# Reordering work around the second chunk of a fused local-attention and gated feed-forward kernel

## The chip, the cores and the metric

The kernel runs on one core of a Trainium2 chip. Its engines are named here as in the profile: PE is TensorE's matmul side and PEld its weight loads, DVE is VectorE, ACT is ScalarE, POOL is GpSimd, SP is SyncE, which here does nothing but issue DMAs. The metric is the device time of one execution in microseconds (us); less is better.

## The reference

Attention over 8 batches, 8 heads, 576 positions and a head width of 64, with a local window and 8 global positions, is followed by a gated feed-forward layer over the 4608 tokens:

```python
scores = scale * np.matmul(q, k.transpose(0, 1, 3, 2))
mask = np.abs(pos[:, None] - pos[None, :]) <= window        # window = 32
mask = mask | is_global[:, None] | is_global[None, :]
attn = softmax(np.where(mask, scores, -1e9))
x = (attn @ v) as 4608 x 512
gelu = 0.5 * g * (1.0 + erf(g * inv_sqrt2))                 # g = x @ w_gate
ffn_out = gelu * (x @ w_val) @ w_out
res_gate = 1.0 / (1.0 + np.exp(-(x @ w_res)))
out = x + res_gate * ffn_out
```

## The kernel before, in words

**Chunks.** The 4608 tokens are cut into 9 chunks of 512 (c = 0 to 8). A chunk is 8 windows of 64 positions, or 4 tiles of 128 tokens (t = 0 to 3). A batch has 9 windows, so chunk c begins in batch c or c-1 and the work for batch b = c + 1 is prepared while chunk c's feed-forward runs. All orders are written out by hand: each engine executes its instructions in the order in which the Python code emits them, so "ahead of" and "behind" below mean places in an engine's own queue. Semaphores are set where one engine's instruction needs another's result or buffer.

**Feed-forward of a chunk.** For each of 12 column blocks j, `ffn_in(c, j)` forms two products of 4 matmuls each (`g_ps`, `v_ps`, L628), takes the Gelu on ACT (L634) and multiplies on DVE (`ht`, L635). Then `ffn_out(c, t)` has, for each of the 4 tiles, a `gate` (4 matmuls into `r_ps`, L646, and a Tanh on ACT into `rsb`, L649) and three `third`s (4 matmuls each into `f_ps`, L671); the last third ends with a DVE step `prb` (L675), a POOL step `ob` (L677) and the DMA of the result from SP (L679).

**Attention of the next chunk, in between.** `scores(c, quad, pps)` forms the scores of four windows and half of the heads (`heads`, L532), takes their exponentials on ACT (`weigh`, L539) and returns a function `mask` that multiplies by the window mask on DVE into `pt` (L555). For chunk 1 alone the exponentials stay in the PSUM bank of the scores (`stay`), and the mask step is what empties that bank. `global_scores(b)`, `global_exp(b)` and `global_rows(b)` treat the 8 global positions of a batch: the last one forms `sn` on PE (L507, L510) from `ptg` and spreads it on DVE into `vgs` (L512). `values(c, t)` forms `nd` for one tile (`local_values`, L573, then the global part from `gt` and `vgs`, L585) and divides on DVE into `xtok` (L591 and L592 for halves, L597 and L598 for whole tiles). `turn_x` transposes `xtok` into `xt`, on PE (L608) or by a DMA from SP (L604).

**PSUM.** Pool `psm` (tag "mm") has four banks that are handed out in turn; `g_ps`, `v_ps`, `r_ps`, `f_ps` and the scores of the second half of the heads share them. Pool `pss` has two banks (scores of the first half of the heads, transposes). Pool `psn` has one buffer of two banks for `sg`, `sn` and `nd`, so a new `nd` waits until the DVE has read the one before.

**Order at the end of chunk 0.** In the last block of the code chunk 1's attention is woven into chunk 0's `ffn_out` by hand: two score groups of quad 0 around `global_scores(1)`, `global_exp(1)`, the gates of tiles 0 and 1 each with its Tanh, the scores of quad 1 and the two other gates alternating, `global_rows(1)`, and the last masks. Then come `values(1, t)` and the thirds. The q and k of batch 2 come in as fp32 into spare space (`load_second`) and are cast to `k_st` on ACT and to `q_st` on POOL (`cast_second`, L205): one piece, then two, then two more of `q_st` at three places among the thirds. `turn_qk(2, "k")` transposes `k_st` into `kt` by DMAs from SP (L466).

**Order at the start of chunk c.** `turn_qk(b)` issues on SP the DMA transposes of `q_st` into `qt` and `k_st` into `kt`; `load_v(b)` (L99) issues five DMAs from POOL's queue; and for c = 1, 2 and 4 `gather` (L328) issues three indirect DMAs from POOL's queue, which fetch the global rows of a pair of batches into `kgf`, `qgf` and `vgf`. At block j = 8 `load_qk(b + 1)` (L91) issues ten DMAs from POOL's queue into `q_st` and `k_st`, each of which waits until the transposes have read its place. In odd chunks, at blocks 8 and 9, `double_qk` (L397), `turn_globals` (L407) and `spread_v` (L435) use what was gathered: pair 1 in chunk 1, pair 2 in chunk 3, pair 3 in chunk 5. At j = 11 `global_scores(b)` uses `qt` and `kt` (`sg` L472, `ss` L481).

**Batch 0.** `local_values(0, 0)` and `local_values(0, 1)` are emitted ahead of `global_rows(0)`; `values(0, 0)` and `values(0, 1)` behind it add the global part.

Of the kernel before, what the change touches and what calls it, by code (L numbers as in the profile page):

```python
# [12 lines left out]
ACTF = mybir.ActivationFunctionType  # L13
# [3 lines left out]
def view(t, p0, pn, off, dims):  # L17

    step = t.ap[0][0]
    return bass.AP(tensor=t.tensor, offset=t.offset + p0 * step + off, ap=[[step, pn]] + dims)  # L20
# [3 lines left out]
def kernel(  # L24
# [12 lines left out]
    nc = tc.nc  # L37
# [459 lines left out]
    def global_rows(b):  # L497

        e = b % 2
        if b:  # L500
            sn = psn.tile([128, 2, 512], F32, name="sn", tag="nd")[:, 0, 0:2 * VG]
        else:
            sn = pss.tile([128, 2 * VG], F32, name="sn", tag="sc")
        for c in range(-1, 5):
            for p in range(NP):
                if c < 0:
                    nc.tensor.matmul(sn[32 * p:32 * p + 32, :], own[e][:, 32 * p:32 * p + 32],  # L507
                                     view(vgb, 0, 128, (b // 2) * VG, [[0, 2], [1, VG]]), start=True, stop=False)
                else:
                    nc.tensor.matmul(sn[32 * p:32 * p + 16, :], ptg[e][:, c, 16 * p:16 * p + 16],  # L510
                                     ve[e][:, c, 2 * p:2 * p + 2, :], start=False, stop=(c == 4))
        nc.vector.tensor_tensor(view(vgs, 0, 128, e * H * VG, [[2 * VG, NP], [VG, 2], [1, VG]]),  # L512
                                view(sn, 0, 128, 0, [[0, NP], [VG, 2], [1, VG]]),
                                view(head8, 0, 128, 0, [[2, NP], [1, 2], [0, VG]]), ALU.mult)


    def first_scores(quad, pp):
# [102 lines left out]
    def ffn_steps(c, j):  # L620
# [15 lines left out]

        return {"g": product("g", wg_t), "v": product("v", wv_t), "end": end}

    def ffn_out(c, t):

        held = {}

        def gate():
            r_ps = psm.tile([128, 512], F32, name="r_ps", tag="mm")
            for kk in range(NKT):
                nc.tensor.matmul(r_ps, xt[c % 2][:, kk, 128 * t:128 * t + 128], wr_t[:, kk, :],  # L646
                                 start=(kk == 0), stop=(kk == NKT - 1))
            held["r"] = work.tile([128, 512], BF16, name="rsb", tag="rsb", bufs=4)
            nc.scalar.activation(held["r"], r_ps, ACTF.Tanh, bias=0.0, scale=0.5)  # L649

        def ending():

            r0 = 512 * c + 128 * t
            for c0, c1 in ((0, 256), (256, 384), (384, 512)):
                f = psm.tile([128, 512], F32, name="f_ps", tag="mm")
                for j in range(NFF):
                    nc.tensor.matmul(f[:, 0:c1 - c0], ht[:, j, 128 * t:128 * t + 128], wo_t[:, j, c0:c1],
                                     start=(j == 0), stop=(j == NFF - 1))
                prb = work.tile([128, 512], F32, name="prb", tag="prb")
                nc.vector.scalar_tensor_tensor(prb[:, c0:c1], held["r"][:, c0:c1], 1.0, f[:, 0:c1 - c0],  # L660
                                               ALU.add, ALU.mult)
                ob = work.tile([128, 512], F32, name="ob", tag="ob", bufs=4)
                nc.vector.tensor_tensor(ob[:, c0:c1], prb[:, c0:c1], xtok[c % 2][:, t, c0:c1], ALU.add)
                nc.sync.dma_start(out[r0:r0 + 128, c0:c1], ob[:, c0:c1])

        def third(n):
            def emit():
                if n == 0:
                    held["f"] = psm.tile([128, 512], F32, name="f_ps", tag="mm")
                for j in range(4 * n, 4 * n + 4):  # L670
                    nc.tensor.matmul(held["f"], ht[:, j, 128 * t:128 * t + 128], wo_t[:, j, :],  # L671
                                     start=(j == 0), stop=(j == NFF - 1))
                if n == 2:
                    prb = work.tile([128, 512], F32, name="prb", tag="prb")
                    nc.vector.scalar_tensor_tensor(prb, held["r"], 1.0, held["f"], ALU.add, ALU.mult)  # L675
                    ob = work.tile([128, 512], F32, name="ob", tag="ob", bufs=4)
                    nc.gpsimd.tensor_tensor(ob, prb, xtok[c % 2][:, t, :], ALU.add)  # L677
                    r0 = 512 * c + 128 * t
                    nc.sync.dma_start(out[r0:r0 + 128, :], ob)  # L679
            return emit  # L680

        if c == NCH - 1 and t == 3:
            return [gate, ending, lambda: None, lambda: None]
        return [gate, third(0), third(1), third(2)]


# [103 lines left out]
    for c in range(NCH):  # L790
        b = c + 1
        if b < B and c:
            turn_qk(b, "q" if c == 1 else "qk")
            load_v(b)
            if c in (1, 2, 4):
                for what in "kqv":
                    gather(what, c // 2 + 1)
        held = None
        for j in range(NFF):
            if c or j > 1:  # L800
                ffn_in(c, j, turns.get(j) if c == 0 else None)
            if c == 0:
                if j == 0:
                    mask_rows(0, NW)
                elif j == 1:
                    mask_rows(NW, NWM)
                    zero_k(1)
                elif j == 2:
                    zero_gt(1, nc.vector)
                    zero_globals(1)  # L810
                    for n in range(1, B // 2):
                        nc.vector.tensor_single_scalar(idx[:, n:n + 1], idx[:, 0:1], float(2 * H * S * n), ALU.add)
                elif j == 3:
                    zero_v(1, nc.vector)
                elif j == 4:
                    double_qk(0, 1)
                elif j == 6:
                    got = turn_globals(0, 1)
                    for what in "kq":
                        DVE(compact[what][:, 0:1, :], got[what])  # L820
                    spread_qk(1, compact, 0, {"k": DVE, "q": ACT})
                elif j == 5:
                    for p in (0, 1, 2, 3, -1):
                        for what in "kq":
                            cast_pair(1, p, what, POOL)
                    load_vraw(1)
                    for n in (14, 15):
                        load_piece(n)
                    for n in (12, 13):
                        cast_piece(n, POOL)  # L830
                    for n in range(16, 20):
                        load_piece(n)
                    for c5 in range(5):
                        cast_v(1, c5, POOL)
                    shift_on_chip(0, POOL)
                    for n in range(14, 20):
                        cast_piece(n, POOL)
                    shift_on_chip(3, POOL)
                if j == 10:
                    turn(3)  # L840
            elif b < B:
                if c % 2 == 1:
                    n0, n1 = b // 2, b // 2 + 1
                    if j == 8:
                        double_qk(n0, n1)
                    elif j == 9:
                        got = turn_globals(n0, n1)
                        for what in "kq":
                            DVE(compact[what][:, n0:n1, :], got[what])
                        spread_v(n0, n1)  # L850
                if j == 8:
                    shift_v(b)
                    if b + 1 < B:
                        load_qk(b + 1)
                if j == 9:
                    spread_qk(b, compact, (b // 2) * 128, {"k": DVE, "q": DVE})
                if j == 11:
                    held = global_scores(b)
        work_f = [w for t in range(4) for w in ffn_out(c, t)]
        if c == 0:  # L860
# [4 lines left out]
            got = global_scores(1)  # L865
            scores(1, 0, (1,))(0, 2)
            global_exp(1, *got)
            work_f[0]()
            work_f[4]()
            scores(1, 1, (0,))(0, 2)  # L870
            work_f[8]()
            mask = scores(1, 1, (1,))
            work_f[12]()
            global_rows(1)
            mask(0, 2)
            for n in (1, 2):
                shift_on_chip(n, ACT)
            for what in "kq":
# [12 lines left out]
            cast_second("q", 0, 1, POOL)  # L891
            values(1, 3)
            third(1, 1)
            cast_second("q", 1, 3, POOL)
            turn_x(1, 2)
            third(2, 1)
            third(3, 1)
# [1 line left out]
            for t in range(4):  # L899
                third(t, 2)  # L900
                if t == 1:
                    cast_second("q", 3, NQT, POOL)
                    turn_qk(2, "k")
            continue
        jobs = {n: [] for n in range(16)}
        if c + 1 < NCH:
# [48 lines left out]
```

## Time and profile before

| what | value |
|---|---|
| median of 9 runs | 396.23 us (395.51 to 396.89) |
| the profiled execution: its own time | 396.27 us |
| its span in the trace | 394.6 us |
| PE busy | 377.0 us (96%) |
| DVE busy | 203.8 us (52%) |
| ACT busy | 170.8 us (43%) |
| POOL busy | 168.5 us (43%) |
| granted TensorE clock | 0.999 of full speed |
| moved by DMA | 52.78 MB |

The trace is one execution; all its times are counted from the start of the span. A timeline row gives the start, the length of the group, the engine, the source line and the operation, and in brackets how long the engine had been idle before it and which instruction ended that idle time. A row of waits gives the total, the number of times and the longest. Matmuls overlap, so the length of a group of matmuls reaches a little beyond the start of the next.

### The profile page before, as it was taken

Reading aid. Unit: us, or ns where it says so; the run is one execution under the profiler, and the core shown is the slowest. Engines: PE = TensorE matmul, PEld = TensorE weight load, DVE = VectorE, ACT = ScalarE, POOL = GpSimd, SP = SyncE. Lnnn points to the kernel's source line nnn. Section 1 sums busy time; section 2 is a strip of 40 time slices with the busy share of each in tenths; the row PEclk is TensorE's granted clock in tenths of the full one; section 3 lists DMA queues with packets and bytes.
Section 4 is the critical chain, followed back from the end, with each engine's and each line's share of the span. In section 5 each row is a group of like instructions: output and inputs, shape, how many; then the busy total and the mean of one; then the engine's idle time right before and its main releaser. Section 6 shows DMA issues by size and latency. Waiting matters only on the chain.

```text
span 394.6 us, 8431 instructions
## 1 busy us (share of the span) xinstructions
PE 377.0 (96%) x3310; PEld 197.4 (50%) x3360; DVE 203.8 (52%) x445; ACT 170.8 (43%) x284; POOL 168.5 (43%) x203
## 2 busy tenths in 40 slices
PE   3989989999999999999999999999999999999996
PEld 2674545444644455445544554455445544554444
DVE  7768674536644563366434553565445534453423
ACT  6663595136333633354234623372336233633321
POOL 7878773858257524461486126712501210121012
PEclk9999999999999999999999999999999999999999
DMA  8999999499749943998299939992990310031002
GB/s 256 271 380 347 233 343 201 98 191 156 89 110 147 189 61 106 119 197 85 80 153 158 123 81 114 191 103 73 125 158 5 93 55 0 2 85 63 0 29 81
DMA packets 153002, 52.78 MB, mean 134 GB/s; under 512 B 136386, under 2 KB 143426, under 8 KB 152962
## 3 DMA queue, kind: packets, MB, share of 16 engines
q1 hardware_dynamic: 77024, 41.88, 45.4%
q0 software_dynamic: 75392, 9.84, 43.0%
q8 instruction: 26, 0.43, 0.5%
q10 hardware_dynamic: 546, 0.52, 0.4%
q14 instruction: 14, 0.11, 0.1%
HBM read 39.19 MB, written 9.44 MB: 123 GB/s over the span
## 4 chain that ended last, share of the span: by engine, by line
PE 75%; DMA 14%; SPq 3%; issue 2%; POOL 2%; DVE 1%; ACT 1%; ACTq 0%; DVEq 0%; POOLq 0%
PE f_ps L671 21%; PE v_ps L628 19%; PE g_ps L628 18%; PE r_ps L646 6%; DMA extra<-in_moe_w_val_dram 5%; PE nd L573 4%; SPq L185 2%; DMA extra<-in_moe_w_out_dram 2%; PE nd L585 2%; PE sc L532 2%; DMA wo_t<-in_k_dram 2%; DMA kt<-k_st 2%; DMA qgf<-in_q_dram,idx 2%; DMA xtok<-in_v_dram 2%; DMA ht<-in_q_dram 1%
## 5 line engine op out<-in xcount | busy, mean ns | idle before, releaser
L635 DVE SCALAR_TENSOR_TENSOR ht<-gsb,v_ps 128x512 bf16<-128x512 bf16 x108 | 74.1, 687 | 97.3 <-PE v_ps L628 86.7
L634 ACT ACTIVATE gsb<-g_ps 128x512 bf16<-128x512 f32 x108 | 64.4, 597 | 125.2 <-PE g_ps L628 110.5
L677 POOL TENSOR_TENSOR ob<-prb,xtok 128x512 f32<-128x512 f32 x35 | 40.4, 1155 | 174.1 <-DVE prb L675 174.1
L628 PE MATMUL v_ps<-xt,wv_t 128*128 128x512 bf16 (+1 forms) x456 | 111.9, 368 | 0.4
L628 PE MATMUL g_ps<-xt,wg_t 128*128 128x512 bf16 (+1 forms) x438 | 109.5, 367 | 0.6
L671 PE MATMUL f_ps<-wo_t,ht 128*128 128x512 bf16 x395 | 97.9, 379 | 1.8 <-issue 0.8
L628 PEld LDWEIGHTS <-wv_t 128*128 128x128 bf16 x456 | 43.5, 98 | 49.1
L628 PEld LDWEIGHTS <-wg_t 128*128 128x128 bf16 x456 | 43.3, 98 | 48.9 <-issue 0.4
L671 PEld LDWEIGHTS <-ht 128*128 128x128 bf16 x420 | 38.9, 98 | 38.7
L649 ACT ACTIVATE rsb<-r_ps 128x512 bf16<-128x512 f32 x36 | 21.7, 608 | 71.0 <-PE r_ps L646 69.9
L675 DVE SCALAR_TENSOR_TENSOR prb<-rsb,f_ps 128x512 f32<-128x512 bf16 x35 | 24.0, 685 | 27.4 <-PE f_ps L671 24.1
L646 PE MATMUL r_ps<-wr_t,xt 128*128 128x512 bf16 x137 | 36.2, 379 | 0.6 <-DVE pt L555 0.2
L539 ACT ACTIVATE pt<-sc 128x512 bf16<-128x512 f32 x64 | 33.3, 614 | 5.2 <-PE sc L532 5.2
L91 POOL DMA_DIRECT2D q_st<-in_q_dram x25 | 21.4, 870 | 20.7 <-DMA qt<-q_st 20.0
L555 DVE TENSOR_TENSOR pt<-pt,maskw 128x512 bf16<-128x512 bf16 x56 | 23.2, 424 | 7.7 <-ACT pt L539 5.8
L573 PEld LDWEIGHTS <-pt 128*128 128x128 bf16 x576 | 21.9, 97 | 10.2 <-issue 1.5
L99 POOL DMA_DIRECT2D ve<-in_v_dram x30 | 25.5, 864 | 0.0
L598 DVE TENSOR_TENSOR xtok<-nd,rden 128x512 bf16<-128x512 f32 x34 | 23.5, 691 | 1.3
L573 PE MATMUL nd<-ve,pt 128*128 128x65 bf16 x320 | 22.5, 193 | 1.5 <-DVE vgs L512 0.9
L91 POOL DMA_DIRECT2D k_st<-in_k_dram x25 | 21.1, 868 | 4.4 <-DMA kt<-k_st 3.0
L597 DVE RECIPROCAL rden<-nd 128x8 f32<-128x8 f32 x34 | 7.0, 207 | 29.3 <-PE nd L585 29.2
L646 PEld LDWEIGHTS <-xt 128*128 128x128 bf16 x144 | 13.5, 97 | 15.3 <-issue 0.2
(172 smaller groups left out, 310.2 us busy)
## 6 DMA issues: line engine op xcount, KB each, us to landing
out_dram<-ob SPq DMA_DIRECT2D x35, 256.0 KB
vo<-ve SPq DMA_DIRECT2D x12, 260.0 KB
q_st<-in_q_dram POOLq DMA_DIRECT2D x20, 128.0 KB, 5.2
k_st<-in_k_dram POOLq DMA_DIRECT2D x20, 128.0 KB, 6.4
ve<-in_v_dram POOLq DMA_DIRECT2D x18, 128.0 KB, 7.4
wo_t<-in_k_dram SPq DMA_DIRECT2D x8, 256.0 KB
vraw<-in_q_dram SPq DMA_DIRECT2D x8, 256.0 KB
extra<-in_moe_w_out_dram SPq DMA_DIRECT2D x4, 512.0 KB
```

The costliest lines, as they stand in the source:

```text
L91: nc.gpsimd.dma_start(dst[0:n, r, :].rearrange("p (h d) -> p h d", d=D), src[b].rearrange("h s d -> s h d")[128 * r:128 * r + n])
L99: nc.gpsimd.dma_start(t[p0:p1, c, :, 0:D], v[b].rearrange("h s d -> s h d")[s0 + p0:s0 + p1])
L539: nc.scalar.activation(sc if stay else mine, sc, ACTF.Exp, bias=0.0, scale=SCALE)
L573: nc.tensor.matmul(nds[h // 4][:, VG * (h % 4):VG * (h % 4) + VG], view(pt, 0, 128, c0, [[1, 128]]), vw, start=(h % 4 == 0 and e == 0), st ...
L598: nc.vector.tensor_tensor(xtok[c % 2][:, t, :].rearrange("p (a h d) -> p a h d", a=2, d=D), num[:, :, :, 0:D], view(rden, 0, 128, 0, [[4, ...
L628: nc.tensor.matmul(held[what][:, c0:c1], w[:, kk, 128 * j:128 * j + 128], x[:, kk, c0:c1], start=(kk == 0), stop=(kk == NKT - 1))
L634: nc.scalar.activation(gsb, held["g"], ACTF.Gelu, bias=0.0, scale=1.0)
L635: nc.vector.scalar_tensor_tensor(ht[:, j, :], gsb, 0.5, held["v"], ALU.mult, ALU.mult)
L646: nc.tensor.matmul(r_ps, xt[c % 2][:, kk, 128 * t:128 * t + 128], wr_t[:, kk, :], start=(kk == 0), stop=(kk == NKT - 1))
L671: nc.tensor.matmul(held["f"], ht[:, j, 128 * t:128 * t + 128], wo_t[:, j, :], start=(j == 0), stop=(j == NFF - 1))
L675: nc.vector.scalar_tensor_tensor(prb, held["r"], 1.0, held["f"], ALU.add, ALU.mult)
L677: nc.gpsimd.tensor_tensor(ob, prb, xtok[c % 2][:, t, :], ALU.add)
```

## The change

It has four parts.

1. `global_rows` writes `vgs` for batch 0 in two halves (two DVE instructions over 4 of the 8 heads each); for the other batches it stays one instruction.
2. At the end of chunk 0, a `gate` can now be emitted without its Tanh. The matmuls of gates 0 and 1 stay where they were; their two Tanhs go behind the first and the second pair of quad 1's exponentials. Quad 1's scores follow one another; `global_rows(1)` comes directly behind them, ahead of quad 1's masks; the gates of tiles 2 and 3 come last, behind `global_rows(1)`.
3. The gathers of pairs 2 and 3 (in chunks 2 and 4) move from the start of the chunk, between `load_v` and `load_qk`, to block 8, behind `load_qk`. Pair 1's gathers stay.
4. Four of the five casts of batch 2's `q_st` on POOL move from among the thirds to behind the last `ob`.

```diff
-        nc.vector.tensor_tensor(view(vgs, 0, 128, e * H * VG, [[2 * VG, NP], [VG, 2], [1, VG]]),
-                                view(sn, 0, 128, 0, [[0, NP], [VG, 2], [1, VG]]),
-                                view(head8, 0, 128, 0, [[2, NP], [1, 2], [0, VG]]), ALU.mult)
+        n = NP if b else NP // 2
+        for p in range(0, NP, n):
+            nc.vector.tensor_tensor(view(vgs, 0, 128, e * H * VG + 2 * VG * p, [[2 * VG, n], [VG, 2], [1, VG]]),
+                                    view(sn, 0, 128, 0, [[0, n], [VG, 2], [1, VG]]),
+                                    view(head8, 0, 128, 2 * p, [[2, n], [1, 2], [0, VG]]), ALU.mult)
...
+    gates = []
+
     def ffn_out(c, t):
...
-        def gate():
+        def gate(now=True):
...
-            nc.scalar.activation(held["r"], r_ps, ACTF.Tanh, bias=0.0, scale=0.5)
+            held["r_ps"] = r_ps
+            if now:
+                open_gate()
+
+        def open_gate():
+            nc.scalar.activation(held["r"], held["r_ps"], ACTF.Tanh, bias=0.0, scale=0.5)
...
+        if c == 0:
+            gates.append((gate, open_gate))
...
-            if c in (1, 2, 4):
+            if c == 1:
                 for what in "kqv":
-                    gather(what, c // 2 + 1)
+                    gather(what, 1)
...
                     if b + 1 < B:
                         load_qk(b + 1)
+                    if c in (2, 4):
+                        for what in "kqv":
+                            gather(what, c // 2 + 1)
...
             global_exp(1, *got)
-            work_f[0]()
-            work_f[4]()
-            scores(1, 1, (0,))(0, 2)
-            work_f[8]()
-            mask = scores(1, 1, (1,))
-            work_f[12]()
+            for t in range(2):
+                gates[t][0](now=False)
+            first = scores(1, 1, (0,))
+            gates[0][1]()
+            second = scores(1, 1, (1,))
+            gates[1][1]()
             global_rows(1)
-            mask(0, 2)
+            first(0, 2)
+            for t in range(2, 4):
+                gates[t][0]()
+            second(0, 2)
...
             cast_second("q", 0, 1, POOL)
             values(1, 3)
             third(1, 1)
-            cast_second("q", 1, 3, POOL)
...
                 if t == 1:
-                    cast_second("q", 3, NQT, POOL)
                     turn_qk(2, "k")
+            cast_second("q", 1, NQT, POOL)
```

## The prediction

> **What bounds the kernel now.** I read the busy table first, then PE's waits, then windows cut at the chunk borders, then the timeline of each place that the change touches.
>
> ```profile
> PE 377.0 (96%) x3310; PEld 197.4 (50%) x3360; DVE 203.8 (52%) x445; ACT 170.8 (43%) x284; POOL 168.5 (43%) x203
> ```
> ```profile
> PE nd L573 <- DVE vgs L512: 0.9, 1, 0.9
> ...
> PE nd L585 <- DVE vgs L512: 0.8, 1, 0.8
> ...
> PE ss L481 <- DMA kt<-k_st: 0.6, 1, 0.6
> ```
> PE is busy for all but 17.6 us, most of that before 25 us (PE busy 16.71 of 25). From there PE runs nearly without a break, so what shortens or lengthens a gap in PE moves the end by as much, and work moved on other engines counts only if PE comes to wait for it. Three of PE's waits lie where the change works: 0.8 (batch 0's `vgs`), 0.9 (batch 1's) and 0.6 (chunk 4's `kt`).
>
> The borders of chunks 2 to 6 are the last twelve `f_ps` matmuls of each chunk:
>
> ```profile
> 110.78:151.48 40.70, 40.27 (x350) 20.44 (x354) 20.11 (x39) 17.02 (x29) 20.34 (x23) 1.00 1.16 125
> 151.48:192.18 40.70, 40.28 (x350) 20.45 (x355) 21.50 (x45) 17.13 (x29) 17.29 (x20) 1.00 1.28 123
> 192.18:233.51 41.33, 40.31 (x349) 20.48 (x354) 19.72 (x39) 16.92 (x29) 20.23 (x23) 1.00 1.20 120
> 233.51:274.21 40.70, 40.28 (x349) 20.31 (x354) 21.32 (x44) 17.01 (x29) 17.16 (x20) 1.00 1.13 124
> ```
> The first number behind the colon is the stretch's length. Chunks 2, 3 and 5 take 40.70 us, chunk 4 takes 41.33. So all that is to be had in parts 3 and 4 of the change is 0.63 us; the rest must come from before 62 us.
>
> **The sum.** I count against the profiled execution, 396.27 us (span 394.6 and 1.67 around it); the median 396.23 lies 0.04 lower.
>
> *Part 1, `vgs` of batch 0 in halves.* DVE's timeline:
>
> ```profile
> 20.89 0.70 DVE L512 TENSOR_TENSOR vgs<-sn,head 128x520 bf16<-128x520 f32 x1 [0.29 <-PE sn L510]
> 21.95 0.18 DVE L591 RECIPROCAL rden<-nd 128x4 f32<-128x4 f32 x1 [0.36 <-PE nd L585]
> 22.17 0.42 DVE L592 TENSOR_TENSOR xtok<-nd,rden 128x256 bf16<-128x256 f32 x1
> 22.51 0.17 DVE L591 RECIPROCAL rden<-nd 128x4 f32<-128x4 f32 x1
> ```
> PE starts `nd` L585 at 21.64, just behind `vgs`; the first reciprocal waits for it, and from 21.95 to 23.98 DVE has no gap; PE's `nd` of tile 3 starts at 24.04, behind DVE's `xtok` of tile 1. So this stretch is a DVE chain. The half has no row of its own; the nearest is L592 (256 wide, also from PSUM): 0.42 long, the next starting 0.34 after it. With it the first half is ready at 21.31 instead of 21.59, the first `nd` and the first reciprocal come 0.28 earlier, and so does everything in the chain: -0.28. The second half ends at 20.89 + 0.34 + 0.42 = 21.65, 0.06 later than now, and its `nd` is ready at 22.01, before DVE asks for it (at 22.23): hidden; uncovered it would cost those 0.06. Ends: 0 (the gap at 24.04 stays) and -0.30.
>
> [...]
>
> *Part 2, the second chunk.* The rows of ACT, DVE and PE from 54 us:
>
> ```profile
> 54.06 1.16 ACT L649 ACTIVATE rsb<-r_ps 128x512 bf16<-128x512 f32 x2
> 55.01 1.18 ACT L539 ACTIVATE sc<-sc 128x512 f32<-128x512 f32 x2
> 56.00 0.69 ACT L649 ACTIVATE rsb<-r_ps 128x512 bf16<-128x512 f32 x1
> ```
> ```profile
> 56.94 0.69 DVE L512 TENSOR_TENSOR vgs<-sn,head 128x520 bf16<-128x520 f32 x1
> 57.55 1.28 DVE L555 TENSOR_TENSOR pt<-sc,maskw 128x512 bf16<-128x512 f32 x2
> 58.81 0.21 DVE L597 RECIPROCAL rden<-nd 128x8 f32<-128x8 f32 x1
> ```
> ```profile
> 57.68 0.64 PE L573 MATMUL nd<-ve,pt 128*128 128x65 bf16 x16 [0.94 <-DVE vgs L512]
> ```
> ACT has no gap from 51.23 to 57.9, so its order is the clock of this stage. A pair of exponentials takes 0.99 of it and a Tanh 0.48; a Tanh's result is there 0.69 after its start.
>
> What goes: the wait for `vgs`. `sn` now follows quad 1's scores. These need the banks that masks 3 and 4 empty (DVE, until 54.33), so they run at 54.4, `sn` (0.53) follows until about 55.5, and DVE, free at 55.55 after the global mask, has `vgs` at 56.24, 1.4 earlier.
>
> What comes instead: `psm` hands its four banks out in turn. Gates 0 and 1 hold two of them until their Tanhs; quad 1's scores take the two others; so gates 2 and 3 take the banks of gates 0 and 1. Before, gate 3 waited for Tanh 1 as well, but that stood ahead of the exponentials (done 55.22, gate 3's matmuls at 55.27). Now ACT runs: exponentials 54.06, Tanh 0 at 55.04, exponentials 55.52, Tanh 1 at 56.50, its result 57.19. Gate 2 starts at 55.78, gate 3 at 57.24; it takes 0.86; queued behind it in PE are `nd` of tile 0 and all that follows. That `nd` starts at 58.10 instead of 57.68: +0.42. DVE no longer sets it: `vgs` and four masks end at 55.55 + 5 x 0.61 = 58.6, before `nd` is ready (58.10 + 1.13). Ends: -0.26, if gate 3 did not hold PE, as the DVE chain would then reach `xtok` at 58.84 instead of 59.10; and +0.60, if each of the nine ACT steps took 0.02 more, as the slower pairs here do. I take +0.42: the order and the banks are fixed, and every duration has a row. Behind this stage PE follows itself; the casts of `k_st` wait for their loads until 61.65 and hide ACT's later end (Tanh 3, then four copies of 0.63, at about 61.2).
>
> *Part 3, gathers of pairs 2 and 3 behind the loads.* In chunk 4 PE has `ss` from 215.66 to 216.22 and then waits to 216.82 for `kt`. POOL there:
>
> ```profile
> 201.17 1.05 POOL L328 DMA_INDIRECT kgf<-in_k_dram,idx  x1 [0.30 <-issue]
> ...
> 204.80 1.91 POOL L91 DMA_DIRECT2D q_st<-in_q_dram  x2
> ```
> The chain of waits goes through `qgf` (6.22 us to landing) to SP's transposes and `kt` (6.74). Chunks 3 and 5, with no gathers, have no such wait, so I take -0.60. But chunk 2 has the same three gathers and no wait either: its `ss` runs at 134.38 in one piece. So the gathers are not the only cause; ends 0 and -0.63. [...]
>
> The three gathers take 3.9 us of POOL behind the last load (chunk 3's ends at 175.5, its first `ob` comes at 181.44): 2 us are to spare, and `prb` has a second buffer. Their data is used a chunk later. Cost nothing; without that cover an `ob` would be late by the overrun.
>
> *Part 4, casts last.* After the first cast POOL is free sooner, but `ob` 1 still waits for `prb` at 71.0, and `ob` 2 and with it the `kt` transposes (SP, 74.27) stay. The `qt` transposes start at 82.00, behind `kt` and two results; the casts end near 77.8. Covered. On POOL two casts (2 x 0.58) move ahead of `load_v(2)`, which goes from 76.56 to 77.7, and pair 1's gathers from 81.18 to 82.4. PE wants their result (`tg` L407) at 89.89; DVE's casts of it ran at 89.04 without a wait. I take 0; ends 0 and +2 (below).
>
> Sum: -0.28 + 0.42 - 0.60 + 0 = -0.46: 396.27 - 0.46 = 395.81, and 395.8 for the median. A measurement of this kernel can tell about 0.2% (0.8 us) from no change, so this is a gain inside that bound.
>
> **Rivals.**
> - *The second chunk pays.* If gate 3 is not what PE waits for, the DVE chain sets the stage (-0.26) and the sum is -0.28 - 0.26 - 0.60 = -1.14: 395.1. For it: DVE's chain from 51.85 to 59.79 has only one gap, of 0.19. Against it: the banks. Chance 0.25.
> - *Part 3 does not do what it says.* The `kt` wait of chunk 4 stays, or comes in chunk 2. Sum -0.28 + 0.42 = +0.14: 396.4. For it: chunk 2 as above. Chance 0.15.
> - *Slower: pair 1's gathers land too late.* A gather of k lands 7.0 to 7.5 us after its issue; issued at 82.4 that is 89.4 to 89.9, and DVE needs 0.35 for both casts, so `tg` may start at 90.2 instead of 89.89. It decides from a landing after about 89.5. If the later loads also meet the `qt` transposes and stretch as `kt` in chunk 4 did (its last transpose 6.74 us), up to 2 us are lost: net -0.1 to +1.5, 396.2 to 397.8. Against it: DVE had it without a wait at 89.04, so the landing was earlier than that. Chance 0.12.
>
> **How the numbers follow.** The forecast has 0.48. Faster by over 0.2% (under 395.4) needs the first rival, or the forecast with part 2 at half its price: 0.22 + 0.08 = 0.30. Slower by over 0.2% (over 397.0) is the last rival's upper part and what I have not seen: 0.11. The remaining 0.59 is within 0.2%. The range runs from the first rival (395.1) to the middle of the last (396.8); its far end and the lower bounds together are left out.
>
> **What would show it.** Right: `nd` L585 of batch 0 about 0.3 sooner; in the second chunk no wait for `vgs`, but waits of `r_ps` for ACT's `rsb`, with `nd` L573 0.4 later relative to the first exponential; chunk 4 at 40.70; `tg` without a wait. Wrong: a second chunk that ends sooner, chunk 2 or 4 above 40.8, a wait of `tg` L407 for DVE near 90 us, or `ob` late behind the gathers.

## The result, and the profile after

The changed kernel takes 399.21 us (median of 10 runs, 397.65 to 400.33) against 396.23 of the kernel before: ratio 1.0076, 95% interval 1.0064 to 1.0088. The forecast was 395.8, in the range 395.1 to 396.8, so it was wrong, and on the wrong side. The profiled execution took 398.93 us (span 397.2).

The busy table and PE's list of waits say little: PE is busy for 1.8 us more, the wait for `kt` is gone as forecast, and the new wait of `r_ps` for ACT is the forecast one.

```profile
PE 378.8 (95%) x3309; PEld 197.9 (50%) x3360; DVE 201.3 (51%) x446; ACT 171.3 (43%) x284; POOL 168.5 (42%) x203
```
```profile
PE nd L575 <- DVE vgs L514: 1.0, 1, 1.0
...
PE r_ps L650 <- ACT rsb L658: 0.5, 1, 0.5
PE nd L587 <- DVE vgs L514: 0.5, 1, 0.5
...
PE sn L510 <- issue: 0.5, 1, 0.5
```

Each trace has 3360 weight loads. Laid side by side, one by one, they show where the distance between the two kernels changes. It is -0.4 us behind batch 0's `vgs` (-0.12 of it from before that place), between +1.0 and +1.1 from the end of the second chunk's attention to 111 us, and +2.66 at the end. Cut at the first weight load of the last twelve `f_ps` of a chunk, the chunks 2 to 4 are (stretch, length, PE's busy time first):

```profile
111.70:153.69 41.99, 40.93 (x353) 20.66 (x355) 19.70 (x39) 17.23 (x29) 20.19 (x23) 1.00 1.06 121
153.69:194.27 40.58, 40.16 (x351) 20.36 (x355) 21.10 (x44) 17.01 (x29) 17.23 (x20) 1.00 1.25 123
194.27:236.11 41.84, 40.42 (x351) 20.45 (x355) 20.22 (x39) 17.12 (x29) 20.42 (x23) 1.00 1.27 120
```
With the same cuts the kernel before has 40.69, 40.58 and 41.45. So 1.3 us are lost in chunk 2; chunk 4 loses 0.4, though its wait for `kt` is gone; the rest of the loss lies in the second chunk. Three places, then.

**The second chunk: half clock.** Windows of 3.41 us, the granted clock third from the end:

```profile
52.08:55.49 3.41, 1.90 (x58) 1.27 (x58) 2.86 (x6) 3.41 (x9) 3.00 (x5) 0.99 0.85 292
55.49:58.90 3.41, 3.19 (x12) 1.27 (x12) 2.48 (x5) 1.90 (x4) 2.55 (x3) 0.51 1.06 400
```
From 55.44 to 58.85 the clock is halved (the rows are cut 0.05 us late). PE's rows show it: six matmuls of gates 2 and 3 take 2.77 us, about 0.43 apart, where four take 1.02 elsewhere.

```profile
55.37 0.55 PE L650 MATMUL r_ps<-wr_t,xt 128*128 128x512 bf16 x1 [0.54 <-ACT rsb L658]
56.13 2.77 PE L650 MATMUL r_ps<-wr_t,xt 128*128 128x512 bf16 x6 [0.22 <-issue]
```

**Chunks 2 and 4: late results.** ACT's, PE's and POOL's timeline in chunk 2:

```profile
137.13 0.60 ACT L658 ACTIVATE rsb<-r_ps 128x512 bf16<-128x512 f32 x1
138.99 1.08 ACT L541 ACTIVATE pt<-sc 128x512 bf16<-128x512 f32 x2 [1.26 <-PE sc L534]
140.63 1.09 ACT L541 ACTIVATE pt<-sc 128x512 bf16<-128x512 f32 x2 [0.55 <-remote]
```
```profile
136.94 0.64 PE L534 MATMUL sc<-qt,kt 64*128 64x64 bf16 x32
137.52 1.90 PE L680 MATMUL f_ps<-wo_t,ht 128*128 128x512 bf16 x8
139.35 0.24 PE L507 MATMUL sn<-vgb,own 128*32 128x130 bf16 x4
139.42 0.57 PE L510 MATMUL sn<-ve,ptg 128*16 128x130 bf16 x10
140.48 0.41 PE L510 MATMUL sn<-ve,ptg 128*16 128x130 bf16 x10 [0.49 <-issue]
```
```profile
136.22 1.06 POOL L328 DMA_INDIRECT kgf<-in_k_dram,idx  x1 [0.31 <-issue]
137.58 1.01 POOL L328 DMA_INDIRECT qgf<-in_q_dram,idx  x1 [0.30 <-issue]
138.90 0.95 POOL L328 DMA_INDIRECT vgf<-in_v_dram,idx  x1 [0.30 <-issue]
```
The scores are through at 137.6, yet ACT gets the first at 138.99 and the third at 140.63; PE itself stands still for 0.49 with nothing to wait for. It happens while the three gathers run, which part 3 has put there. Chunk 4 has the same at 220 to 224.6 us.

### The profile page after: what moved, and what is told of

Same layout as the page of the kernel before. It is cut to its first block, busy times and chain, and to the rows that moved or that the text cites. A ratio compares the mean times of both kernels' runs of the same rounds, so it can differ in the third digit from the quotient of the medians.

```text
span 397.2 us, 8437 instructions
## 1 busy us (share of the span) xinstructions
PE 378.8 (95%) x3309; PEld 197.9 (50%) x3360; DVE 201.3 (51%) x446; ACT 171.3 (43%) x284; POOL 168.5 (42%) x203
## 4 chain that ended last, share of the span: by engine, by line
PE 80%; DMA 11%; SPq 2%; ACT 2%; POOL 1%; issue 1%; DVE 1%; ACTq 0%; another core or an unknown queue 0%; DVEq 0%
PE v_ps L630 21%; PE f_ps L680 21%; PE g_ps L630 20%; PE r_ps L650 6%; PE nd L575 4%; DMA extra<-in_moe_w_val_dram 3%; PE sc L534 2%; DMA extra<-in_moe_w_out_dram 2%; SPq L185 2%; PE nd L587 2%; DMA wo_t<-in_k_dram 2%; DMA ht<-in_q_dram 2%; DMA vraw<-in_v_dram 1%; DMA xtok<-in_v_dram 1%; ACT pt L541 1%
## 5 line engine op out<-in xcount | busy, mean ns | idle before, releaser
L650 PE MATMUL r_ps<-wr_t,xt 128*128 128x512 bf16 x135 | 37.5, 391 | 1.1 <-ACT rsb L658 0.5
```

## The experiments

**Theories.** A: the gathers among the scores delay PE's results by themselves. B: the second chunk's order is the cause of all, through PE's idle time and shifted loads. C: both depend on something outside the kernel. Sixteen runs were made in four more comparisons, each with the kernel before on the same chip; the first comparison is that of the result. Part numbers are the prediction's. Each median is of 6 to 12 executions. The lengths of chunks 2 and 4 are cut as above, from the one execution of each run that was traced.

| run | parts | median, us | ratio to before (95%) | chunk 2 | chunk 4 |
|---|---|---|---|---|---|
| first: after | 1 2 3 4 | 399.21 | 1.0076 (1.0064 to 1.0088) | 41.99 | 41.84 |
| second: p1_halves | 1 | 396.45 | 1.0014 (1.0001 to 1.0026) | 40.69 | 41.82 |
| p14_halves_casts | 1 4 | 394.93 | 0.9969 (0.9957 to 0.9982) | 40.70 | 41.20 |
| p2_chunk | 2 | 396.90 | 1.0014 (1.0001 to 1.0027) | 40.70 | 41.98 |
| p3_gathers | 3 | 395.12 | 0.9973 (0.9964 to 0.9983) | 40.70 | 40.69 |
| third: p134_no_second | 1 3 4 | 395.04 | 0.9976 (0.9964 to 0.9989) | 40.69 | 40.69 |
| p124_no_gathers | 1 2 4 | 396.31 | 1.0008 (0.9993 to 1.0024) | 40.69 | 41.18 |
| p234_no_halves | 2 3 4 | 396.32 | 1.0016 (1.0000 to 1.0032) | 40.70 | 40.69 |
| after_again | 1 2 3 4 | 396.75 | 1.0016 (1.0001 to 1.0030) | 40.69 | 41.08 |
| fourth: after_third | 1 2 3 4 | 398.75 | 1.0065 (1.0041 to 1.0090) | 42.19 | 42.19 |
| after_fill | all, and PE work | 397.99 | 1.0047 (1.0030 to 1.0063) | 42.70 | 42.01 |
| tanh_first | 1 3 4, half of 2 | 397.46 | 1.0042 (1.0025 to 1.0059) | 41.79 | 41.70 |
| p4_casts | 4 | 394.99 | 0.9971 (0.9959 to 0.9983) | 40.70 | 40.69 |
| fifth: p3_again | 3 | 398.55 | 1.0060 (1.0044 to 1.0076) | 42.19 | 42.05 |
| pool_copies | 1 4, POOL copies | 395.46 | 0.9976 (0.9965 to 0.9987) | 40.70 | 41.03 |
| plain_loads | 1 4, plain loads | 395.27 | 0.9978 (0.9965 to 0.9991) | 40.70 | 40.69 |
| tanh_no_gathers | 1 4, half of 2 | 394.65 | 0.9961 (0.9945 to 0.9978) | 40.69 | 40.69 |

One of the 6 executions of after_third took 1007.17 us, which no trace explains; without it the median is 398.72.

### Parts alone (second comparison)

Each is the kernel before with the hunks of the diff that the table names.

> Part 1 alone (batch 0's vgs in two halves). The trace of the changed kernel has PE 0.4 us ahead of before from 23 us on, so all theories: 0.3 to 0.4 us faster than before (395.85), the reciprocal behind the first nd 0.3 earlier. If the gain is taken back before the end, the time is that of before.

> Parts 1 and 4 (halves of vgs, and four casts of batch 2's q behind the last ob). Theory: the casts cost nothing, time as with part 1 alone (395.85). Rival: pair 1's gathers, issued 1.2 us later, stall tg near 90 us, 0.3 to 2 us above part 1 alone.

> Part 2 alone (the order of the second chunk). Theory 1 (gate 3 waits for Tanh 1, and the wait lets the granted clock fall in some executions): +0.4 us in executions at full clock, +1.4 to 1.7 in executions whose mean clock is 0.995 or 0.996; median of all 0.4 to 1.0 above before. Rival: the half-clock spell comes from elsewhere (part 1 or 4 moved the idle gaps), then +0.4 in all executions, mean clock 0.999.

> Part 3 alone (gathers of pairs 2 and 3 behind the loads). Theory 1 (an indirect DMA issued while the scores and sn are under way makes PE's results reach ACT and DVE 1 to 2 us late): chunk 2 loses about 1.0, chunk 4 gains 0.6 to 0.75 and loses 1.1, net +1.3 to +1.5 us. Rival (the late results in chunks 2 and 4 come with the other parts, which shifted the stage in time): -0.6, chunk 4 at 40.70.

Parts 1 and 2 alone lose a little, parts 3, and 1 with 4, gain about 0.3% each. Part 1 alone was expected at 395.85 and missed that. In its trace the first reciprocal does come 0.79 us after the start of `vgs` instead of 1.06, but the gain is lost again further on. Part 3 alone has no late result at all, which spoke against A as I then had it. Parts 1 and 2 show what part 4 is for. POOL's and DVE's rows of part 1 alone:

```profile
68.91 0.61 POOL L205 CAST q_st<-vraw 128x512 bf16<-128x512 f32 x1 [4.56 <-DMA vraw<-in_q_dram]
71.09 0.61 POOL L205 CAST q_st<-vraw 128x512 bf16<-128x512 f32 x1 [1.58 <-DMA vraw<-in_q_dram]
72.15 0.62 POOL L205 CAST q_st<-vraw 128x512 bf16<-128x512 f32 x1 [0.44 <-DMA vraw<-in_q_dram]
72.73 2.27 POOL L679 TENSOR_TENSOR ob<-prb,xtok 128x512 f32<-128x512 f32 x2
```
```profile
73.92 0.69 DVE L677 SCALAR_TENSOR_TENSOR prb<-rsb,f_ps 128x512 f32<-128x512 bf16 x1 [2.36 <-POOL ob L679]
```
```profile
74.66 1.02 PE L630 MATMUL g_ps<-xt,wg_t 128*128 128x512 bf16 x4 [0.37 <-DVE prb L677]
```
The casts wait for their loads, `ob` stands behind the casts, `prb` waits for `ob`, and PE for the bank that `prb` empties. Chunk 1, 40.74 us in before, takes 41.69 in this trace and 41.33 in that of part 2 alone. In the trace of before the second cast ran 2.8 us earlier (at 68.30) and nothing of this was to be seen; nor in the two traces of part 3 alone (68.26 and 68.34), which have the old order of casts too. Why the loads came late in two of these five traces is not shown.

### Each part left out (third comparison)

Against the changed kernel:

```diff
-            for t in range(2):                         # p134_no_second: the old order
-                gates[t][0](now=False)
...
+            work_f[0]()
+            work_f[4]()
...
-            if c == 1:                                 # p124_no_gathers
+            if c in (1, 2, 4):
...
-        n = NP if b else NP // 2                       # p234_no_halves
+        n = NP
```

> All of the change but part 2: the second chunk keeps its old order. Theory A (the loss belongs to the new order of the second chunk: it holds gates 2 and 3 behind ACT, costs the half-clock spell, and pushes the loads of later chunks against PE): no half clock near 55 us, no late results in chunks 2 and 4, no wait for kt in chunk 4; 394.93 (parts 1 and 4) less 0.6 to 0.8 for the wait, so 394.1 to 394.4. Theory B (the loss belongs to the gathers behind the loads, whatever the second chunk does): ACT's exponentials wait about 1 us in chunks 2 and 4 here too, and the time is 396 to 397.

> All of the change but part 3: the gathers of pairs 2 and 3 stand ahead of the loads as before. Theory A: the second chunk costs 0.4 to 0.6 and in some executions 1 us more at half clock, the wait for kt in chunk 4 stays or grows to 1: 396.0 to 397.5. Theory B: without the gathers in the stretch of the scores nothing is late; 394.93 plus 0.4 = 395.3 to 395.6.

> All of the change but part 1: one vgs of full width in batch 0. Both theories give part 1 about 0.3 of gain by itself, so 399.2 plus 0.3 = 399.5 if the late results come whatever the first stage does. If it is only how PE's stages and the loads happen to fall against each other that makes them late, a shift of 0.3 us can end it: 397 or less.

> The changed kernel once more, for a second trace. If the half clock near 55 us and the late results of chunks 2 and 4 (ACT's first exponential of the chunk 1.2 us after its scores, vgs 2 us after sn) belong to the kernel, they stand in this trace at the same instructions, and the median is again 399.2. If they belong to one execution, this trace lacks one or both and ends where it lacks them 1 to 2 us earlier.

The changed kernel itself takes 396.75 here, 2.5 us less than in the first comparison, with before unchanged (396.08). Its late results are gone:

```profile
110.76:151.45 40.69, 40.27 (x351) 20.47 (x355) 20.72 (x39) 17.01 (x29) 20.20 (x23) 1.00 1.14 125
...
192.03:233.11 41.08, 40.43 (x352) 20.51 (x355) 20.27 (x39) 17.04 (x29) 20.45 (x23) 1.00 1.27 123
```
So they don't belong to the kernel alone: B fell for chunks 2 and 4, and C held in part. This trace also had the full clock in the second chunk, so it shows part 2 by itself:

```profile
55.48 1.02 PE L650 MATMUL r_ps<-wr_t,xt 128*128 128x512 bf16 x3 [0.54 <-ACT rsb L658]
56.96 1.02 PE L650 MATMUL r_ps<-wr_t,xt 128*128 128x512 bf16 x4 [0.46 <-ACT rsb L658]
57.82 0.65 PE L575 MATMUL nd<-ve,pt 128*128 128x65 bf16 x16
```
From ACT's `gt` to `nd` of tile 0 it is 4.58 us here and 4.15 in before: +0.43. What is left is the clock: 7 of the 11 executions had a mean granted clock of 0.994 to 0.996, and these took 396.97 us on average; the other four, at 0.998 and more, took 395.65. One window of 3.41 us at half clock lowers the mean by 3.41 x 0.5 / 397 = 0.004, so these are executions with one such window, and it costs 1.3 us (1.1 to 1.7 in the four other kernels that have several of them).

Leaving part 2 out gives 395.04, which neither theory expected (394.1 to 394.4, or 396 to 397); leaving out part 3 or part 1 is worth nothing measurable beside these swings.

### What halves the clock, what part 4 is worth, and the fourth comparison

Against the changed kernel again: in after_fill PE goes twice through `sn`; in tanh_first, gates 0 and 1 have their Tanh at once:

```diff
-        for c in range(-1, 5):
+        for c in [*range(-1, 5)] * (2 if b == 1 else 1):       # after_fill
```
```diff
-                gates[t][0](now=False)
+                gates[t][0]()                                   # tanh_first
             first = scores(1, 1, (0,))
-            gates[0][1]()
             second = scores(1, 1, (1,))
-            gates[1][1]()
```

> The changed kernel once more, beside the next three on one chip. Two comparisons of it gave 399.2 and 396.75 us. In the first one's trace PE's results reach ACT and DVE about 1 us late in chunks 2 and 4, and landing records are missing around every group of gathers (in the trace of before from that comparison too); in the second nothing is late and no record is missing there. Theory: the late results belong to the place of measurement and not to the kernel, so 396.5 to 397 here, of which about 1.3 us times the share of executions with half clock. Rival: they belong to the kernel and come at random; then some comparisons, this one perhaps, show 398 to 399 again.

> The changed kernel, but PE goes through batch 1's 24 sn matmuls twice (the second pass starts the sums anew, so the result is the same): 0.53 us of PE work is put into its idle time ahead of gate 2. Window theory: the clock is halved for 3.41 us when PE was busy for less than some 2.2 of the 3.41 us of the window before; the traces have half clock after windows with 1.90 and 2.13 us, none after 2.37 and more. With the fill no window falls below 2.3: no execution at clock 0.996 or less, and 395.4 to 395.8, the time of the changed kernel's executions at full clock. Rival: the half clock has another cause (the order on ACT, or chance); it stays in about half of the executions: 396.7 or, with the added work, 397.2.

> The changed kernel with one piece of part 2 undone: Tanh 0 and Tanh 1 stand ahead of quad 1's exponentials again, the global rows stay ahead of the second masks. If gates 2 and 3 wait only because their banks are held until Tanh 0 and 1, PE's two waits (0.54 and 0.46) go, nd of tile 0 comes at 56.8 instead of 57.8, DVE's masks then end last and the stage is 0.6 to 0.8 sooner; PE has no window under 2.3 us, so no half clock: 394.7 to 395.2, faster than both kernels. Rival: ACT sets the stage; the exponentials come 0.96 later with the Tanhs ahead of them, and the stage ends as it did in the kernel before: 395.6 to 396.0.

> Part 4 alone. The prediction gave it nothing. New theory: in the old order POOL's second and third cast wait for their loads, ob stands behind them, prb waits for ob and PE's g_ps for prb (0.3 to 0.8 us lost at 74 us in the traces of parts 1 and 2 alone, nothing where the loads come early as in the trace of before). With the casts last this cannot happen: 395.0 to 395.5, and no wait of g_ps for prb. If part 4 is worth nothing: 396.1.

*Clock.* The records of the clock lie on a grid of 3.41 us (in after, full clock from 14.48 to 55.44 us is 12 steps of it, the half clock to 58.85 one) whose place differs from one execution to the next (full clock starts between 11.98 and 15.14 us in these traces). The theory was that PE's busy time in the grid's own window decides. The row of p124_no_gathers that was followed by a halved window, then the two of after_fill, in which nothing was halved:

```profile
52.00:55.41 3.41, 2.08 (x59) 1.21 (x58) 2.86 (x6) 3.41 (x10) 3.15 (x5) 0.99 1.00 358
55.41:58.82 3.41, 3.01 (x7) 1.17 (x8) 2.78 (x5) 2.21 (x5) 3.09 (x5) 0.51 1.08 378
```
```profile
51.95:55.36 3.41, 2.24 (x83) 1.55 (x82) 2.76 (x6) 3.41 (x9) 3.30 (x4) 1.00 1.02 368
55.36:58.77 3.41, 2.95 (x29) 1.70 (x29) 2.91 (x5) 2.76 (x6) 3.05 (x4) 1.00 1.11 360
```
After 1.90 (after) and 2.08 us (2.14 on the exact grid) of PE work in 3.41 the clock was halved; in the second chunk it never was after 2.24 and more. In the order of part 2 the emptiest window that a grid could cut there is 1.84 to 1.90 us; in the old order it is 2.2. But the sum of busy time isn't the rule. Elsewhere, windows on the grid with as little work were followed by full clock: 1.97 us at 20.39 in p2_chunk (and at 20.38 in p234_no_halves), 2.10 at 134.86 in p3_again (and at 135.08 in after_third).

```profile
20.39:23.80 3.41, 1.97 (x35) 1.54 (x35) 2.90 (x9) 2.74 (x4) 3.15 (x6) 1.00 1.01 339
23.80:27.21 3.41, 3.41 (x69) 3.38 (x66) 1.85 (x6) 1.17 (x2) 1.51 (x2) 1.00 1.05 397
```
```profile
134.86:138.27 3.41, 2.10 (x40) 1.20 (x38) 0.84 (x2) 2.48 (x6) 1.38 (x2) 1.00 1.46 118
138.27:141.68 3.41, 3.41 (x60) 1.85 (x60) 2.54 (x7) 1.65 (x4) 0.61 (x1) 1.00 0.00 0
```
What sets the two halved windows apart is open. They hold 59 matmuls, most of them small (scores of 64 rows, `sn` of 16 columns); these two hold 35 and 40.

That it is part 2's order is shown: 23 of 65 executions with the whole of it have a clock of 0.996 or less, none of 93 of the kernels without it, and none of the 113 of the kernel before in these four comparisons (after_fill and tanh_first, which change part 2's order, are not among the 65 or the 93). The fill is weaker evidence: all of after_fill's seven executions had 0.998 or more, but only one of six of after_third beside it had less; if the fill did nothing, seven of seven had a chance of (42/65)^7, or 5%. The prediction of "no half clock" for tanh_first was a miss: 2 of 12 executions had 0.996. Its trace has no second-chunk window below 2.4 us, so the cause of these two is open. The late results below also empty PE, but p3_again has them with the old second chunk, and none of its six executions has less than 0.998.

The halved window of after lies behind one in which PE's longest gap was 0.54 us and its gaps together 1.5 of the 3.41 us: here the half clock came without a longer gap.

*Part 4* alone gains 0.3%: only the first cast still stands ahead of an `ob`, and in its trace chunk 4's wait for `kt` is gone as well. With part 4 and the gathers in their old place, chunk 4 takes 40.69 us in three traces and 41.03 to 41.20 in three; with neither part 3 nor part 4, 41.45 to 41.98. Why a move at 75 us shortens a wait at 216 is not shown.

*The late results are back* in after_third, and in tanh_first and after_fill (in the latter's trace PE stands still for 1.47 us in chunk 2). What sets this comparison and the first apart from the second and third could be read in the traces. Where none is missing, a DMA's arrival has left 16 records at its semaphore (in before, 192 for the 12 DMAs of one semaphore; its 284 DMAs would make 4544). In all traces of the first and fourth comparison such records are missing, many of them around the gathers, and in the kernel before too: 4261 to 4358 are left. In the second and third there are 4516 to 4530. The fourth ran on chip 13, the second and third on chips 10 and 11; the first's chip is not on record. Against the times expected without late results (up to 397, 395.8 and 395.2), after_third, after_fill and tanh_first are 1.8 to 2.3 us longer.

### Is it the gathers? (fifth comparison)

What was open by then was what makes the results late. The control is part 3 alone; two kernels on parts 1 and 4 keep the gathers in the old place and put something else into the new one:

```diff
                         load_qk(b + 1)
+                    if c in (2, 4):                             # pool_copies
+                        for _ in range(5):
+                            nc.gpsimd.tensor_copy(pad, wr_t[:, 0, :])
```
```diff
+                        for i, src in enumerate((k, q, v)):     # plain_loads
+                            nc.gpsimd.dma_start(pad[:, i, :], src.rearrange("b h s d -> (b h s) d")[128 * c:128 * c + 128])
```

> Part 3 alone once more, as a control beside the next three. In the two comparisons in which landing records are missing around the gathers, the kernels with gathers among the scores lost about 1 us in chunk 2 and again in chunk 4; in the two others none was lost. If records are missing in this comparison's traces: late results in chunks 2 and 4, 396.3 to 397.2 (395.1 and some 1.5 to 2). If none are missing: 395.1 as before. A rival in which the late results belong to the second chunk's new order, and not to the gathers, expects 395.1 in either case.

> Parts 1 and 4, the gathers in their old place; where part 3 puts them, five POOL copies of a weight tile to a spare tile (about 3 us of POOL, no DMA). If it is POOL's being busy there that makes PE's results late, this loses what the control loses: 396 to 397. If it is the indirect DMA: 394.9 to 395.1 whatever the control does.

> Parts 1 and 4, the gathers in their old place; where part 3 puts them, three plain loads on POOL's queue of 128 rows of 64 from k, q and v to a spare tile (the same bytes as the gathers). If any DMA from POOL's queue at that place makes results late, this loses what the control loses: 396 to 397. If it takes the indirect form: 394.9 to 395.2.

> The best that the runs point to: parts 1 and 4, of part 2 the global rows ahead of the second masks but Tanh 0 and 1 ahead of the exponentials, and the gathers in their old place (part 3 undone). Against parts 1 and 4 (394.93) the second chunk gives 0.5 to 0.8: 394.1 to 394.5, in any comparison, faster than both kernels. If a second chunk with global rows ahead is not worth anything once the clock stays whole: 394.9.

It ran on chip 13 again, and records were missing again (4248 to 4374 are left; 4455 in plain_loads, whose six added loads bring 96). Part 3 alone, 395.12 in the second comparison, now takes 398.55, more than the 396.3 to 397.2 expected. Its PE stands still within the scores for 1.31 us, while `kgf` (132.93 to 133.99) has passed and `qgf` and `vgf` are being issued; the second fence is the same code on chip 10:

```profile
134.66 0.20 PE L532 MATMUL sc<-qt,kt 64*128 64x64 bf16 x1
136.18 0.62 PE L532 MATMUL sc<-qt,kt 64*128 64x64 bf16 x31 [1.31 <-issue]
```
```profile
135.08 0.64 PE L532 MATMUL sc<-qt,kt 64*128 64x64 bf16 x32
135.66 1.90 PE L671 MATMUL f_ps<-wo_t,ht 128*128 128x512 bf16 x8
```
Five POOL copies (4.0 us of POOL) and three plain loads in the same place, on the same chip, cost nothing there: chunk 2 stays at 40.70 in both. Their medians, 395.46 and 395.27, lie a little above what was expected (up to 395.1 and 395.2); where that comes from is not shown.

```profile
133.57 3.97 POOL L860 COPY pad<-wr_t 128x512 bf16<-128x512 bf16 x5
```
```profile
134.10 0.58 POOL L860 DMA_DIRECT2D pad<-in_k_dram  x1
134.67 0.55 POOL L860 DMA_DIRECT2D pad<-in_q_dram  x1
135.21 0.54 POOL L860 DMA_DIRECT2D pad<-in_v_dram  x1
```
So in these runs it is neither POOL's being busy (395.46) nor a plain load on its queue (395.27): of the three, only the indirect form does it (398.55), and only where records go missing (395.12 where they do not). The cleanest pair differs in the gathers' place alone, on one chip: tanh_first 397.46, tanh_no_gathers 394.65. Part 3 also brings the loads of chunks 2 and 4 nearer to the transposes, but that isn't it: chunk 3 has no gathers, its loads directly follow `load_v`, and it takes 40.58 or 40.59 in every trace. Shown: in three comparisons of five, every kernel with gathers among the scores loses 1.1 to 2.0 us in chunk 2 and 1.0 to 1.5 in chunk 4 (over 40.69), and every kernel with the gathers ahead of `ffn_in` loses nothing in chunk 2, though records are missing around its gathers too. A likely reason, not tested: in `ffn_in` PE, ACT and DVE exchange a result only every 0.86 us and with buffers between them. Not shown either: what an indirect DMA holds up on that chip, whether it is the chip or how it was set up, and whether the missing records and the late hand-offs have one cause.

**The best version**, tanh_no_gathers (parts 1 and 4, Tanhs first, global rows ahead of the second masks, gathers where they were), takes 394.65 us, 0.4% under before, on the chip on which part 3 loses 0.6%. It lies between the 394.1 to 394.5 expected and the 394.9 of the rival, and its interval overlaps that of parts 1 and 4. Gates 2 and 3 find their banks free:

```profile
54.36 0.46 PE L510 MATMUL sn<-ve,ptg 128*16 128x130 bf16 x20
54.74 1.90 PE L650 MATMUL r_ps<-wr_t,xt 128*128 128x512 bf16 x8
56.48 0.65 PE L575 MATMUL nd<-ve,pt 128*128 128x65 bf16 x16
```
From ACT's `gt` (53.10) to this `nd` it is 3.38 us; in before 4.15, in after_again 4.58. At most about 0.3 of the 0.77 reach the median (394.93 for parts 1 and 4, on another chip): the next tile's `nd` waits for `xtok` (1.0 us in two waits, 0.8 before).

## Why the prediction was wrong, step by step

**Part 1** was right in its place: the halves take 0.76 us together, as added up from the row of L592, and PE's wait for the first is 0.5 instead of 0.8 (in after_again it is 0.8 again, as DVE is still at `gt` when `sn` is ready). The gain of 0.28 is not found in the whole, though: part 1 alone is 0.19 slower than before, and part 4 alone and with part 1 are alike (394.99 and 394.93, on two chips).

**Part 2's order** was right: at full clock the second chunk's stretch from `gt` to `nd` of tile 0 is 0.43 longer, 0.42 was forecast, and gates 2 and 3 wait for ACT as forecast. **Its sum lacked a term**: what the new order does to the granted clock. The trace of before had 1.00 in every window, and I took that as given. The term is 1.3 us in the executions it strikes, about a third of them (23 of 65), and 1.0 us in the profiled one.

**Part 3's cover was the step that failed most.** "Cost nothing" counted POOL's time and the landing, and no wait for either shows. The gain was there where nothing disturbed it: chunk 4 at 40.69 instead of 41.45 in three of four traces (41.08 in after_again). But the gathers run while PE, ACT and DVE hand over results at every step, and in the first comparison this cost 1.30 us in chunk 2 and 1.15 in chunk 4 (41.84 against 40.69). The prediction's term for this was 0. The prediction named "chunk 2 or 4 above 40.8" as what would show it wrong; that is where it showed.

**Part 4** was mis-sized: 0 forecast, about -1.2 measured alone. I read one execution, in which the loads came early, and took the order on POOL as harmless; and I did not see that chunk 4's wait shrinks with it too. How the 1.2 divides between the two is not shown. For the same reason the bound of 0.63 us for parts 3 and 4 together was wrong: either alone gains 1.1 to 1.2. The two do not add up: parts 1, 3 and 4 take 395.04, parts 1 and 4 take 394.93.

**The rivals.** The second chunk did not pay in this order (the banks decided, as forecast); part 3 did what it said; `tg` has no wait near 90 us. The mechanism that made the kernel slower was on none of the lists.

**The sum, by the profiled execution.** +1.08 up to chunk 2 (-0.39 behind part 1, the order +0.43 as in after_again, the rest, about 1.0, half clock), +1.30 in chunk 2, +0.39 in chunk 4, -0.11 behind it: +2.66, which is 398.93 - 396.27. Where neither disturbance struck (the trace of after_again, 396.03 us), the same kernel is 0.24 below the profiled execution of before; its four executions at full clock average 395.65, 0.43 under that comparison's 396.08. The forecast was 0.46 below. That this agrees is luck: the gain of part 1 isn't found in the whole, parts 3 and 4 brought about 1.0 and not 0.60, and part 2 took about 0.6 of it back (395.65 against 395.04). One reading at the start of the prediction was off too, without effect on the sum: of PE's 17.6 us of idle time 8.3 lie before 25 us, which is not most.

## What to carry to other kernels

Before an order that leaves PE more holes is called cheap, look at the granted clock of several executions, and sum PE's work over every 3.41 us (the step of the clock's records here) that it touches: windows of 1.9 to 2.1 us of work in the second chunk cost 1.3 us in a third of the executions. A low sum is a warning and not a rule, as windows of 2.0 and 2.1 elsewhere cost nothing. Look at what the engines do while an indirect DMA runs, even if its own time and its data have slack: three of them among the scores cost 1.1 to 2.0 us in chunk 2 in three comparisons of five, ahead of `ffn_in` nothing there; missing arrival records, in the profile of before too (4358 of some 4520), went with the loss in all three comparisons that have it. And taking casts that wait for their loads from ahead of an output step was worth 1.2 us (part 4 alone, 394.99 against 396.22), though the one profiled execution of before shows no wait of PE there.

## What the runs showed of the hardware

- The time at which the clock first goes full differs by up to 3.2 us between executions (11.98 to 15.14 us; 14.95 in before, 14.48 in after). In the traces of before and after, the weight loads of `tk` and `tq` in a row start 0.11 us apart ahead of it and 0.06 behind it, and the 100th weight load starts between 13.55 and 14.85 us over all traces. So absolute times of two of these traces differ by up to 1.3 us there already, while chunk 3 takes 40.58 or 40.59 us in every trace.
- One window of half clock followed PE gaps of no more than 0.54 us in the trace of after. By their mean clock (0.996 or less), 23 of 65 executions with the whole of part 2 had such a window; the others of the same kernels had 0.998 or more.
- With three indirect DMAs of 128 rows among the scores, PE, ACT and DVE lost 1.0 to 2.0 us a chunk in three comparisons of five: 395.12 and 398.55 us for the same code, on chips 10 and 13, beside a kernel before that stayed at 396.06 to 396.26. Whether it is the chip or how it was set up is not shown.
